# Half of a first MLP stage as seven half-size products instead of eight, with its x sums on VectorE

## Chip, cores and metric

One NeuronCore of a Trainium2 chip runs the whole program. The metric is the device time of one execution in microseconds; the time before is a median of 265.79 us over three runs (265.69 to 265.80). Views and rows call the engines PE (TensorE, matrix products), PEld (its weight loads), DVE (VectorE), ACT (ScalarE), POOL (GpSimd) and SP (SyncE, which here only issues DMAs).

## What is computed

```python
q_s = exp(q - max(q));  q_s /= sum(q_s, axis=-1)          # q, k, v: batch 8, heads 8, seq 576, head_dim 64
k_s = exp(k - max(k));  k_s /= sum(k_s, axis=seq)
kv  = einsum('bhsd,bhse->bhde', k_s, v)
x   = einsum('bhsd,bhde->bhse', q_s, kv)  ->  (8, 576, 512)
xn  = (x - mean(x)) / sqrt(var(x) + 1e-6) * g_ln
out = x + relu(xn @ w_ch1) @ w_ch2                        # w_ch1 (512, 2048), w_ch2 (2048, 512)
```

The output is float32 of shape (8, 576, 512).

## The kernel before

**Chunks.** The 8 x 576 rows of x are worked on in nine chunks of 512 rows: chunk c below 8 is the first 512 rows of batch c, chunk 8 (`C9`) the last 64 rows of all batches. A chunk has four column groups t of 128 rows. Attention gives x (`po_mm` on TensorE, then `x_fast` on VectorE, which scales x, sums it and calls `xn_out`), x is transposed to xnT (in chunk 1 by TensorE and a copy, `xn_pT`; from chunk 2 on by a DMA from SP's queue, `xn_T`), and the MLP follows in two stages. The first stage makes hT, 16 row tiles m of 128 rows, from w1g and xnT with four contraction steps ko; the second makes y from hT and w2.

**Order.** Everything is in a schedule written by hand: each engine executes its instructions in the order in which the program issues them. `run(main, side)` (L775) walks through a chunk's TensorE steps. Each has a weight, 1 for a matmul of 512 columns and 0.5 for one of 256, and before each step `run` issues all side work whose position is at most the weight so far. So "position 51" of chunk 1 means: behind 51 units of its main matmuls. `second_side` (L818) is the side work of chunk 1: the sums of the second weight for later products (`quarter_w2`), what is left of chunk 1 (`square_sum`, `rstd_op`), and the attention of chunk 2 and loads and exponentials of chunk 3. What a main step calls at its own end is issued within that step.

**Seven products.** From chunk 2 on, both stages replace eight products of half-size blocks by seven (a Strassen-Winograd form). `mm1_fast` (L691) does the first stage so: per g (four row tiles of hT, two block rows) seven products of four 256-column matmuls each, for pairs of g in the order 1, 5, 6, 2, 7, 3, 4, each product for both g of a pair before the next. It uses three PSUM banks per g, named x, b and c:

- after product 1, `seed` copies bank x to bank c (ScalarE); after 5, `copy_5` copies b to SBUF (ScalarE); after 6, `add_5` makes b = x + copy (VectorE, L719);
- after 2, a relu of c to hT (ScalarE); after 7, `out_22` writes x + copy to hT (VectorE, L722), for odd g with a maximum with 0 over two g (L727); after 3 and 4, relus of b and x (ScalarE).

Products 6, 7 and 4 add onto bank x, 2 onto c and 3 onto b, so 7 waits until `add_5` has read x, and 4 until `out_22` has. The products need sums of w1's blocks (`sum_w1`, in w1q, parts 0 and 1 for the lower and upper g) and of xnT's (`sum_x` into tq, four sums of two instructions each, L240: on GpSimd, or on VectorE from chunk 7 on).

The second stage `mm2_fast` (L622) does the same with 16 matmuls for each product in the order 1, 5, 6, 2, 7, 3, 4, and needs sums of hT (`sum_h(g, i)`, L528 on VectorE; g = 0 for hT's row tiles 0 to 7, g = 1 for 8 to 15). Product 5 reads sum 0, product 6 sum 1.

**Chunk 1 (`FAST`) before** uses seven products only in its second stage. Its first stage is `mm1_part` for row tiles 0 to 7 (64 matmuls of 256 columns, L451, with relus L462), columns t = 0 and 1 first since t = 3 is transposed at position 8, then `mm1` for row tiles 8 to 15 (32 matmuls of 512 columns, L436, relus L424): 64 units, and 56 for the second stage.

Six PSUM banks belong to the pool `mm_ps`, two to `att_ps` (kv and po).

Of the kernel before, what the change touches and what calls it, by code (L numbers as in the profile page):

```python
# [12 lines left out]
FP32 = mybir.dt.float32  # L13
# [7 lines left out]
def kernel(  # L21
# [16 lines left out]
    nc = tc.nc  # L38
# [5 lines left out]
    T = 4  # L44
# [183 lines left out]
    def sum_x(c, i):  # L228

        if i == 0:  # L230
            tqs[c] = mlp.tile([P, 4, 2, 2, P], BF16, tag="tq", name="tq", bufs=1)
        (b11, b12), (b21, b22) = [
            [xnTs[c][:, 2 * half : 2 * half + 2, 2 * kh : 2 * kh + 2, :] for half in range(2)]
            for kh in range(2)
        ]
        t1, t2, t3, t4 = [tqs[c][:, n] for n in range(4)]
        dst, x, y = ((t1, b12, b11), (t2, b22, t1), (t3, b22, b12), (t4, b21, t2))[i]
        eng = nc.vector if c >= C9 - 1 else nc.gpsimd
        for t in range(2):
            eng.tensor_tensor(out=dst[:, t], in0=x[:, t], in1=y[:, t], op=ALU.subtract)  # L240
# [178 lines left out]

    def relu(i, dst, src, fast):  # L420
        if i % 8 == 7 and not fast:
            nc.vector.tensor_scalar_max(dst, in0=src, scalar1=0.0)
        else:
            nc.scalar.activation(dst, src, AF.Relu)  # L424

    hbox = {}

    def new_h():
        hbox["h"] = mlp.tile([P, KO2, T, P], BF16, tag="hT", name="hT", bufs=1)

    def mm1(c, m, ko):
        if m == 0 and ko == 0:
            new_h()
        if ko == 0:
            hbox["ph"] = mm_ps.tile([P, T, P], FP32, tag="m", name="ph")
        nc.tensor.matmul(  # L436
            hbox["ph"], w1g[:, ko, m * P : (m + 1) * P], xnTs[c][:, :, ko, :],
            start=(ko == 0), stop=(ko == KO1 - 1),
        )
        if ko == KO1 - 1:  # L440
            relu(m, hbox["h"][:, m], hbox["ph"], c >= FAST)

    def mm1_part(c, m, t0, tn, ko):

        if (m, t0, ko) == (0, 0, 0):
            new_h()
        half, at = divmod(t0, 2)
        if m % 2 == 0 and at == 0 and ko == 0:
            hbox["ph", m // 2] = mm_ps.tile([P, 2, 2, P], FP32, tag="m", name="ph")
        ph = hbox["ph", m // 2]  # L450
        nc.tensor.matmul(  # L451
            ph[:, m % 2, at : at + tn], (w1g if c else w1_sb)[:, ko, m * P : (m + 1) * P],
            xnTs[c][:, t0 : t0 + tn, ko, :],
            start=(ko == 0 and m % 2 == 0 and at == 0), stop=(ko == KO1 - 1),
            skip_group_check=True,
        )
        if m % 2 == 1 and at + tn == 2 and ko == KO1 - 1:
            dst = hbox["h"][:, m - 1 : m + 1, 2 * half : 2 * half + 2]
            if c == 0 and half and (m // 2) % 2 == 1:
                nc.vector.tensor_scalar_max(dst, in0=ph, scalar1=0.0)  # L460
            else:
                nc.scalar.activation(dst, ph, AF.Relu)  # L462
# [19 lines left out]

    def mm2(c, t, ko):
        if ko == 0:
            hbox["pc"] = mm_ps.tile([P, DM], FP32, tag="m", name="pc")
        nc.tensor.matmul(
            hbox["pc"], hbox["h"][:, ko, t, :], w2_sb[:, ko, :],
            start=(ko == 0), stop=(ko == KO2 - 1),
        )
        if ko == KO2 - 1:  # L490
            y_out(c, t, hbox["pc"])

    def mm2_stream(c, t, ko):
# [23 lines left out]
    def sum_h(g, i):  # L517

        if g == 0 and i == 0:
            hbox["s"] = mlp.tile([P, 4, KH, 2 * P], BF16, tag="hs", name="hs", bufs=1)  # L520
        ks = slice(KH // 2 * g, KH // 2 * g + KH // 2)
        s1, s2, s3, s4 = [hbox["s"][:, n, ks] for n in range(4)]
        a11, a12, a21, a22 = [h_part(odd, half, ks) for half in range(2) for odd in range(2)]
        dst, x, y, op = (
            (s1, a21, a22, ALU.add), (s2, s1, a11, ALU.subtract),
            (s3, a11, a21, ALU.subtract), (s4, a12, s2, ALU.subtract),
        )[i]
        nc.vector.tensor_tensor(out=dst, in0=x, in1=y, op=op)  # L528

    def prod(n, bank, t, k, first=False, own=False):  # L530

# [10 lines left out]
        else:  # L542
            rhs = w2_q[:, {5: 0, 6: 1, 7: 2, 4: 3}[n], k]
        nc.tensor.matmul(hbox[bank][:, t], lhsT, rhs, start=first and (own or t == 0) and k == 0,  # L544
                         stop=k == KH - 1, skip_group_check=True)
# [76 lines left out]
    def mm2_fast(c):  # L622
# [3 lines left out]
        def product(n, name, first=False, at=None, ts=range(2), own=False, cut=None):  # L626
            at = at or {}
            order = [(t, k) for t in ts for k in range(KH)]
            if cut:
                order = [(t, k) for ks in (range(cut), range(cut, KH)) for t in ts for k in ks]  # L630
            for i, (t, k) in enumerate(order):

                def go(t=t, k=k, i=i):
                    if i == 0 and first:
                        bank(name)
                    prod(n, name, t, k, first or own, own)
                    for fn in at.get(i + KH * ts[0], []):
                        fn()

                steps.append((0.5, go))  # L640
# [16 lines left out]
        def sums(*which):  # L657
            return [lambda g=g, i=i: sum_h(g, i) for g, i in which if g or c == FAST or i > 1]

        product(1, "a", first=True, cut=6, at={  # L660
            0: sums((1, 0), (0, 1), (1, 1)),
            15: [seed_c]})
# [27 lines left out]

    def mm1_fast(c):  # L691

# [44 lines left out]
        )  # L737
        steps.append((0, new_h))
        for g0 in (0, 2):
            for n, name, first, after in plan:  # L740
# [4 lines left out]
    def mlp_steps(c):  # L745
        if c > FAST:
            return mm1_fast(c) + mm2_fast(c)
        full = range(KO2)
        first, parts = [], ()
        if c == 0:  # L750
            full = range(0)
            parts = ((0, 2, 0, 1), (0, 2, 1, 1), (2, 2, 0, 1), (2, 2, 1, 1), (4, 4, 0, 2), (0, 4, 2, 1),
                     (0, 4, 3, 1), (4, 4, 2, 2), (8, 4, 0, 2), (8, 4, 2, 2), (12, 4, 0, 2), (12, 4, 2, 2))
        else:
            full, parts = range(8, KO2), ((0, 8, 0, 2), (0, 8, 2, 2))
        for m0, mn, t0, tn in parts:
# [3 lines left out]
            ]  # L760
        first += [(1, lambda m=m, ko=ko: mm1(c, m, ko)) for m in full for ko in range(KO1)]
        if c == 0:
# [3 lines left out]
            ]  # L766
        if c >= FAST:
            return first + mm2_fast(c)
        return first + [(1, lambda t=t, ko=ko: mm2(c, t, ko)) for t in range(T) for ko in range(KO2)]

# [47 lines left out]
    def second_side():  # L818
# [3 lines left out]
        s += [(3, lambda: exp_q(2, 0, 4)), (7, lambda: exp_q(2, 2, 4)), (7.2, lambda: eq_T(2))]  # L822
        s += [(42, lambda: square_sum(1, 2)), (67, lambda: square_sum(1, 3)), (71, lambda: rstd_op(1))]
        s += [(7.3, lambda: load_batch(3, (2,), eqTs[2][0:1, T - 1, NP - 1, 0:4])), (31, lambda: load_batch(3, (0,)))]
        s += [(9 + 2 * j, lambda j=j: cast_v(2, j)) for j in range(2)]
        s += [(7.4, lambda: load_v(3))]
        s += [(93 + j, lambda j=j: cast_v(3, j)) for j in range(2)]
        s += [(15 + 3 * t, lambda t=t: reduce_q(2, t, 2)) for t in (0, 2)]
        s += [(36, lambda: recip_q(2))]
        s += [(18, lambda: exp_k(2, 0, 4)), (22, lambda: exp_k(2, 2, 4)), (26, lambda: prep_kvrem(2))]  # L830
        s += [(41, lambda: kv_all(2))]
        s += [(46, lambda: start_x(2))]
        for t, (p0, p1) in enumerate(((52, 54), (57, 59), (62, 65), (70, 74))):
            s += spread([lambda t=t, i=i: po_mm(2, t, i) for i in range(NP)], p0, p1)
            s += [(p1, lambda t=t: x_fast(2, t)), ((73, 82, 88, 94)[t], lambda t=t: square_sum(2, t))]
        s += [(60, lambda: xn_T(2, 0, 2)), (77, lambda: xn_T(2, 2, 2)), (100, lambda: rstd_op(2))]
        s += [(75, lambda: exp_q(3, 0, 4)), (79, lambda: exp_q(3, 2, 4)), (85, lambda: eq_T(3))]
        s += [(97, lambda: exp_k(3, 0, 4)), (108, lambda: exp_k(3, 2, 4)), (113, lambda: prep_kvrem(3))]
        s += [(p, lambda i=i: sum_w1(i, 1)) for i, p in ((3, 30),)]
        s += spread([lambda i=i: sum_x(2, i) for i in range(4)], 95, 108)  # L840
        return s
# [184 lines left out]
    with tc.manual_schedule(  # L1026
# [10 lines left out]
        def po_x(c, t):  # L1037
# [25 lines left out]
            + [(p, lambda i=i: sum_w1(i, 0)) for i, p in enumerate((80, 84, 88, 92))]  # L1063
            + [(p, lambda i=i: sum_w1(i, 1)) for i, p in enumerate((96, 98, 100))]
            + [(103 + 0.4 * j, lambda j=j: cast_v(1, j)) for j in range(2)]
# [8 lines left out]
        for c in range(1, B):  # L1074
# [12 lines left out]
            if c == B - 2:  # L1087
                side += [(1, load_qrem)]
                side += spread([lambda r=r: exp_qrem(r) for r in range(T)], 58, 80)
                side += [(84, lambda: eq_T(C9))]  # L1090
            sums = [(57, 0)] if c == FAST else [(p, i) for i, p in enumerate((30, 41))]
            run(mlp_steps(c), side + [(at, lambda i=i: sum_h(0, i)) for at, i in sums])
# [31 lines left out]
```

## Time and profile before

| what | value |
|---|---|
| median of three runs | 265.79 us |
| the profiled execution | 265.6 us |
| its span, first to last instruction | 263.6 us |
| granted TensorE clock, mean | 0.999 |
| chunk 1's matmuls, both stages | 49.37 to 77.47 us |
| first row of the page's slices, PE | 9 of 10 in nearly every slice |

The page's parts are busy times by engine, the span in 40 slices, DMA queues, the chain of work that ended last, the costliest groups of instructions and the DMA issues. A busy PE is not a PE at its peak, since matmuls overlap in the pipeline; what tells is the distance between starts. In the rows "L719" is line 719 of the kernel, "out<-in" gives the tiles by their names in the program, and the bracket at the end of a timeline row is the idle time of the engine ahead of it and what ended it.

### The profile page before, as it was taken

To read this page: it belongs to the slowest core of one execution; us is meant where nothing else is said; L and a number is where in the kernel's file an instruction comes from. 1 tells how busy PE (TensorE), PEld (TensorE's weight loads), DVE (VectorE), ACT (ScalarE), POOL (GpSimd) and SP (SyncE) were. 2 spreads that over 40 slices of the span, in tenths; PEclk is the share of its full clock that TensorE was granted. 3 is DMA by queue.
4 is the path that set the end of the run, shared out by engine and by line. 5 is a ranking of instruction groups with operands and counts; after the bars stand their busy time and mean duration, and the time that the engine had idled before them with its cause. 6 is when DMAs were issued, how large, how long until landed. Compare 5 with 4: busy or idle time off the path is not lost.

```text
span 263.6 us, 6818 instructions
## 1 busy us (share of the span) xinstructions
PE 257.4 (98%) x2708; PEld 218.1 (83%) x2711; DVE 217.4 (82%) x475; ACT 178.8 (68%) x350; POOL 76.0 (29%) x126
## 2 busy tenths in 40 slices
PE   8989999999999999999999999999999999999993
PEld 5778855775988998899889988998899888888882
DVE  4667797968989997989798979997999889877873
ACT  4467852896966888688868886788678377438400
POOL 8652316203049007600760076008200300030000
PEclk9999999999999999999999999999999999999999
DMA  6999999997986995799879957997804620521014
GB/s 219 256 204 208 338 208 315 271 155 233 207 151 197 325 136 97 197 308 155 93 215 298 139 99 237 297 135 146 256 6 79 161 82 12 71 90 72 0 42 119
DMA packets 69847, 45.00 MB, mean 171 GB/s; under 512 B 41460, under 2 KB 66040, under 8 KB 69816
## 3 DMA queue, kind: packets, MB, share of 16 engines
q1 hardware_dynamic: 48896, 21.76, 39.3%
q0 software_dynamic: 20320, 22.29, 38.9%
q10 hardware_dynamic: 600, 0.53, 0.6%
q8 instruction: 21, 0.34, 0.6%
q14 instruction: 10, 0.08, 0.1%
HBM read 36.70 MB, written 9.44 MB: 175 GB/s over the span
## 4 chain that ended last, share of the span: by engine, by line
PE 92%; DMA 4%; POOL 2%; issue 0%; ACT 0%; DVE 0%; POOLq 0%
PE ba L544 21%; PE bx L688 19%; PE bb L688 9%; PE ph L451 8%; PE bb L544 5%; PE be L544 5%; PE bc L544 5%; PE pc L497 5%; PE bc L688 5%; DMA w_raw<-in_moe_w_ch_dram 4%; PE ph L436 3%; PE po L353 3%; PE pkv L316 2%; PE ptr L860 1%; POOL v L931 1%; PE po L360 1%
## 5 line engine op out<-in xcount | busy, mean ns | idle before, releaser
L544 PEld LDWEIGHTS <-hs 128*128 128x128 bf16 x512 | 49.5, 98 | 5.7
L688 PEld LDWEIGHTS <-w_q 128*128 128x128 bf16 x448 | 43.1, 98 | 5.2 <-issue 0.2
L544 PEld LDWEIGHTS <-hT 128*128 128x128 bf16 x384 | 37.2, 98 | 4.4
L240 POOL TENSOR_TENSOR tq<-xnT 128x256 bf16<-128x256 bf16 x20 | 12.9, 661 | 78.6 <-DMA xnT<-xn 47.2
L688 PEld LDWEIGHTS <-w1g 128*128 128x128 bf16 x336 | 32.2, 98 | 3.9
L544 PE MATMUL ba<-w_q,hs 128*128 128x256 bf16 x256 | 31.7, 273 | 0.0
L688 PE MATMUL bx<-tq,w_q 128*128 128x256 bf16 x224 | 29.0, 273 | 0.0
L561 POOL DMA_DIRECT2D out_dram<-ot x28 | 15.3, 557 | 46.4 <-DVE ot L555 46.4
L367 ACT ACTIVATE scrap<-x,mv 128x512 bf16<-128x512 bf16 x36 | 25.9, 719 | 1.7 <-DVE x L383 1.3
L383 DVE SCALAR_TENSOR_TENSOR x<-po,rq 128x512 bf16<-128x512 f32 x34 | 23.3, 685 | 1.2 <-PE po L353 1.1
L712 ACT COPY bc<-bx 128x512 f32<-128x512 f32 x28 | 15.2, 594 | 13.0 <-PE bx L688 13.0
L719 DVE TENSOR_TENSOR bb<-bx,s 128x512 f32<-128x512 f32 x28 | 18.2, 694 | 6.3 <-ACT s L716 6.3
L730 ACT ACTIVATE hT<-bc 128x512 bf16<-128x512 f32 x28 | 15.3, 595 | 11.9 <-PE bc L688 11.9
L202 DVE TENSOR_REDUCE zq<-eq 128x16 f32<-128x1024 bf16 (+1 forms) x20 | 20.6, 1049 | 2.3 <-ACT eq L193 2.3
L528 DVE TENSOR_TENSOR hs<-hT 128x1024 bf16<-128x1024 bf16 x32 | 20.9, 674 | 0.9 <-ACT hT L730 0.5
L730 ACT ACTIVATE hT<-bb 128x512 bf16<-128x512 f32 x28 | 15.2, 595 | 8.8 <-PE bb L688 8.8
L353 PE MATMUL po<-kv_sb,eqT 128*128 128x128 bf16 x120 | 20.5, 219 | 0.0
L722 DVE TENSOR_TENSOR hT<-bx,s 128x512 bf16<-128x512 f32 x28 | 18.0, 684 | 3.0 <-PE bx L688 3.0
L569 ACT COPY s<-ba 128x512 f32<-128x512 f32 x15 | 8.7, 579 | 12.5 <-PE ba L544 7.8
L544 PE MATMUL ba<-w_sb,hT 128*128 128x256 bf16 x128 | 16.7, 273 | 0.0
L544 PE MATMUL bb<-w_q,hs 128*128 128x256 bf16 x128 | 16.6, 273 | 0.0
L497 PE MATMUL pc<-w_sb,hT 128*128 128x512 bf16 x61 | 15.6, 379 | 0.2
(135 smaller groups left out, 536.9 us busy)
## 6 DMA issues: line engine op xcount, KB each, us to landing
out_dram<-ot POOLq DMA_DIRECT2D x32, 256.0 KB, 5.9
qt<-in_q_dram SPq DMA_DIRECT2D x5, 1024.0 KB, 7.1
kt<-in_k_dram SPq DMA_DIRECT2D x5, 1024.0 KB, 15.0
vt<-in_v_dram POOLq DMA_DIRECT2D x7, 512.0 KB, 14.3
w_sb<-in_moe_w_ch_dram POOLq DMA_DIRECT2D x4, 512.0 KB, 16.1
qt<-in_q_dram POOLq DMA_DIRECT2D x2, 1024.0 KB, 14.8
kt<-in_k_dram POOLq DMA_DIRECT2D x2, 1024.0 KB, 14.3
w_raw<-in_moe_w_ch_dram POOLq DMA_DIRECT2D x3, 512.0 KB, 13.1
```

The lines of the kernel that those rows point to most:

```text
L202: nc.vector.reduce_sum(eqs[c][1][:, ts], eqs[c][0][:, ts], axis=AX.X)
L353: nc.tensor.matmul(pobox["p"][:, i * P : i * P + P], eqTs[c][:, t, i, :], kv_sb[:, c, i, :], start=True, stop=True,)
L367: nc.scalar.activation(scrap, x[:, t], AF.Square, bias=mv[:, t, 0:1], scale=-float(DM), accum_out=mv[:, t, 1:2],)
L383: nc.vector.scalar_tensor_tensor(x[:, t].rearrange("p (h d) -> p h d", h=H), in0=pobox[c, t].rearrange("p (h d) -> p h d", h=H), scalar=1. ...
L451: nc.tensor.matmul(ph[:, m % 2, at : at + tn], (w1g if c else w1_sb)[:, ko, m * P : (m + 1) * P], xnTs[c][:, t0 : t0 + tn, ko, :], start=( ...
L497: nc.tensor.matmul(hbox["pc", t], hbox["h"][:, ko, t, :], w2_sb[:, ko, :], start=(ko == 0), stop=(ko == KO2 - 1),)
L528: nc.vector.tensor_tensor(out=dst, in0=x, in1=y, op=op)
L544: nc.tensor.matmul(hbox[bank][:, t], lhsT, rhs, start=first and (own or t == 0) and k == 0, stop=k == KH - 1, skip_group_check=True)
L688: nc.tensor.matmul(dst[:, q], lhsT, rhs, start=first and q == 0 and ko == 0, stop=ko == 1, skip_group_check=True)
L719: nc.vector.tensor_tensor(out=at[g, "b"], in0=at[g, "x"], in1=at[g, "s"], op=ALU.add)
L722: nc.vector.tensor_tensor(out=h_out(g, 1, 1), in0=at[g, "x"], in1=at[g, "s"], op=ALU.add)
L730: nc.scalar.activation(h_out(g, odd, half), at[g, name], AF.Relu)
```

## The change

For chunk 1 alone:

- `mlp_steps`: the first stage computes row tiles 8 to 15 by `mm1_part` (64 matmuls of 256 columns as before, of other rows), and then row tiles 0 to 7 by `mm1_fast(c, (0,))`, one pair of g: 56 matmuls of 256 columns, 28 units. `mm1`, `relu` and `mm2` have no caller left and go.
- x's four sums are issued at position 8.2, on VectorE. tq's sums for chunk 2 stay on GpSimd.
- `sum_h` for g = 1 is issued at 36 and 38, as those row tiles are now ready first; the second stage takes their rows first (`rows`), and the sums for g = 0 follow at its first step.
- Of `second_side`, what lay at 41 or later mostly moves 3 to 4 units sooner, as the first stage is 4 units shorter: `kv_all(2)` 41 to 38.5, `po_mm` and `x_fast` of chunk 2, `xn_T`, `exp_q`, `exp_k`, `cast_v`, `sum_x(2)`, `square_sum(1, 3)`, `rstd_op`. `quarter_w2` at 44 and 46 and `square_sum(1, 2)` at 42 stay.
- The last `sum_w1` of part 1 moves from position 30 of chunk 1 to 105 of chunk 0.

A flag in `prod` (which matmul clears its bank) is passed in another way, with the same effect for the other chunks.

```diff
-        eng = nc.vector if c >= C9 - 1 else nc.gpsimd
+        eng = nc.vector if c >= C9 - 1 or c == FAST else nc.gpsimd
...
-            order = [(t, k) for t in ts for k in range(KH)]
+            rows = [(k + KH // 2) % KH for k in range(KH)] if c == FAST else list(range(KH))
+            order = [(t, k) for t in ts for k in rows]
...
         product(1, "a", first=True, cut=6, at={
-            0: sums((1, 0), (0, 1), (1, 1)),
+            0: sums((0, 0), (0, 1)) if c == FAST else sums((1, 0), (0, 1), (1, 1)),
...
-    def mm1_fast(c):
+    def mm1_fast(c, pairs=(0, 2)):
...
-        for g0 in (0, 2):
+        for g0 in pairs:
...
         else:
-            full, parts = range(8, KO2), ((0, 8, 0, 2), (0, 8, 2, 2))
+            parts = ((8, 8, 0, 2), (8, 8, 2, 2))
...
-        first += [(1, lambda m=m, ko=ko: mm1(c, m, ko)) for m in full for ko in range(KO1)]
...
-        if c >= FAST:
-            return first + mm2_fast(c)
-        return first + [(1, lambda t=t, ko=ko: mm2(c, t, ko)) for t in range(T) for ko in range(KO2)]
+        return first + mm1_fast(c, (0,)) + mm2_fast(c)
...
-        s += [(42, lambda: square_sum(1, 2)), (67, lambda: square_sum(1, 3)), (71, lambda: rstd_op(1))]
+        s += [(42, lambda: square_sum(1, 2)), (63, lambda: square_sum(1, 3)), (67, lambda: rstd_op(1))]
...
-        s += [(93 + j, lambda j=j: cast_v(3, j)) for j in range(2)]
+        s += [(89 + j, lambda j=j: cast_v(3, j)) for j in range(2)]
...
-        s += [(41, lambda: kv_all(2))]
+        s += [(38.5, lambda: kv_all(2))]
         s += [(46, lambda: start_x(2))]
-        for t, (p0, p1) in enumerate(((52, 54), (57, 59), (62, 65), (70, 74))):
+        for t, (p0, p1) in enumerate(((49, 51), (54, 56), (59, 62), (66, 70))):
             s += spread([lambda t=t, i=i: po_mm(2, t, i) for i in range(NP)], p0, p1)
-            s += [(p1, lambda t=t: x_fast(2, t)), ((73, 82, 88, 94)[t], lambda t=t: square_sum(2, t))]
-        s += [(60, lambda: xn_T(2, 0, 2)), (77, lambda: xn_T(2, 2, 2)), (100, lambda: rstd_op(2))]
-        s += [(75, lambda: exp_q(3, 0, 4)), (79, lambda: exp_q(3, 2, 4)), (85, lambda: eq_T(3))]
-        s += [(97, lambda: exp_k(3, 0, 4)), (108, lambda: exp_k(3, 2, 4)), (113, lambda: prep_kvrem(3))]
-        s += [(p, lambda i=i: sum_w1(i, 1)) for i, p in ((3, 30),)]
-        s += spread([lambda i=i: sum_x(2, i) for i in range(4)], 95, 108)
+            s += [(p1, lambda t=t: x_fast(2, t)), ((69, 78, 84, 90)[t], lambda t=t: square_sum(2, t))]
+        s += [(57, lambda: xn_T(2, 0, 2)), (73, lambda: xn_T(2, 2, 2)), (96, lambda: rstd_op(2))]
+        s += [(71, lambda: exp_q(3, 0, 4)), (75, lambda: exp_q(3, 2, 4)), (81, lambda: eq_T(3))]
+        s += [(93, lambda: exp_k(3, 0, 4)), (104, lambda: exp_k(3, 2, 4)), (109, lambda: prep_kvrem(3))]
+        s += spread([lambda i=i: sum_x(2, i) for i in range(4)], 91, 104)
...
-            + [(p, lambda i=i: sum_w1(i, 1)) for i, p in enumerate((96, 98, 100))]
+            + [(p, lambda i=i: sum_w1(i, 1)) for i, p in enumerate((96, 98, 100, 105))]
...
-            sums = [(57, 0)] if c == FAST else [(p, i) for i, p in enumerate((30, 41))]
+            if c == FAST:
+                side += [(8.2, lambda i=i: sum_x(c, i)) for i in range(4)]
+                side += [(p, lambda i=i: sum_h(1, i)) for i, p in enumerate((36, 38))]
+            sums = [] if c == FAST else [(p, i) for i, p in enumerate((30, 41))]
```

## Prediction

> **What bounds the kernel now.** First the page's first part, then the busy time by stage (columns: stretch and its length, then busy time and count of PE, PEld, DVE, ACT, POOL, the granted TensorE clock, DMA share, GB/s). Its first row is chunk 1, its second chunk 2.
>
> ```profile
> PE 257.4 (98%) x2708; PEld 218.1 (83%) x2711; DVE 217.4 (82%) x475; ACT 178.8 (68%) x350; POOL 76.0 (29%) x126
> ```
>
> ```profile
> 49.37:77.47 28.10, 28.10 (x271) 22.10 (x269) 22.97 (x51) 24.05 (x47) 5.25 (x10) 1.00 1.09 209
> 77.47:103.68 26.21, 26.21 (x283) 23.44 (x281) 23.41 (x49) 20.59 (x39) 11.19 (x19) 1.00 0.86 190
> ```
>
> TensorE is busy for the whole of chunk 1, so whether it works or stands is read from the chain of waits (start, length, what). There eight 256-column matmuls take 0.87 us and nine 512-column ones 1.94 us:
>
> ```profile
> 51.34 5.24 PE ph L451 x48
> 56.58 1.94 PE ph L436 x9
> ...
> 79.22 0.87 PE bx L688 x8
> ```
>
> That is 0.109 us for a 256-column matmul, 0.218 us for one unit of the list's weight. 120 units (26.21 us), the 40 small matmuls of kv (0.84), 16 of po (0.87) and four transposes (0.22) make 28.14 us, against 28.10 measured: chunk 1 has no TensorE stall, and the end of the kernel hangs on TensorE's work.
>
> Then VectorE's own timeline in chunk 1, because the change gives VectorE work there (start, length of the merged group, instruction, count, idle time before and its releaser). Groups overlap their neighbours: what an instruction costs its queue is the distance to the next start, which I call its pitch.
>
> ```profile
> 51.38 0.42 DVE L864 COPY xnT<-ptr 128x512 bf16<-128x512 bf16 x1 [0.27 <-PE ptr L860]
> 51.72 0.68 DVE L511 TENSOR_TENSOR w_q<-w_sb 128x1024 bf16<-128x1024 bf16 x1
> 52.32 0.77 DVE L134 COPY vm<-vt 128x1024 bf16<-128x1024 bf16 x2
> 52.99 0.69 DVE L511 TENSOR_TENSOR w_q<-w_sb 128x1024 bf16<-128x1024 bf16 x1
> 53.59 2.34 DVE L202 TENSOR_REDUCE zq<-eq 128x16 f32<-128x1024 bf16 x2
> 55.85 0.75 DVE L226 TENSOR_TENSOR w_q<-w1g 128x512 bf16<-128x512 bf16 x2
> 56.52 0.35 DVE L804 RECIPROCAL rq<-zq 128x32 f32<-128x32 f32 x1
> ...
> 59.32 0.18 DVE L325 RECIPROCAL rzk<-pkv 128x4 f32<-128x4 f32 x1 [2.45 <-PE pkv L316]
> 59.54 0.86 DVE L327 TENSOR_TENSOR kv_sb<-pkv,rzk 64x256 bf16<-64x256 f32 x2
> 60.43 1.42 DVE L511 TENSOR_TENSOR w_q<-w_sb,w_q 128x1024 bf16<-128x1024 bf16 x2
> 62.45 0.69 DVE L383 SCALAR_TENSOR_TENSOR x<-po,rq 128x512 bf16<-128x512 f32 x1 [0.61 <-PE po L353]
> ```
>
> The reader sees two holes, 2.45 and 0.61 us. The rows that the added work is priced by stand in later chunks, and one on ScalarE:
>
> ```profile
> 56.86 1.13 ACT L462 ACTIVATE hT<-ph 128x512 bf16<-128x512 f32 x2
> ...
> 79.75 1.30 DVE L719 TENSOR_TENSOR bb<-bx,s 128x512 f32<-128x512 f32 x2 [0.23 <-ACT s L716]
> ...
> 82.30 1.29 DVE L722 TENSOR_TENSOR hT<-bx,s 128x512 bf16<-128x512 f32 x2 [0.28 <-PE bx L688]
> 83.63 0.70 DVE L727 TENSOR_SCALAR hT<-hT 128x1024 bf16<-128x1024 bf16 x1
> ...
> 205.14 0.49 DVE L240 TENSOR_TENSOR tq<-xnT 128x256 bf16<-128x256 bf16 x2 [0.87 <-DMA xnT<-xn]
> ```
>
> **TensorE's part.** 32 matmuls of 512 columns (weight 32) go, 56 of 256 columns (weight 28) come: 4 units, 4 x 0.218 = 0.87 us less. Without a new wait the median would be 265.79 - 0.87 = 264.92.
>
> **Work that lies beside other work.** ScalarE loses eight L424 and gets ten copies and relus of the same size (0.59 us); walked on from 57.82 (the pitch after the L462 pair) the two seeds and two copies of product 5 end at 59.9, while VectorE first wants them at 60.3: hidden with 0.4 us to spare; without that cover a delay would pass one to one into `add_5` and on to TensorE. The last `sum_w1` (two instructions, 0.67) goes into VectorE's 0.85 us wait for pkv ahead of 42.85: nothing, and 0.67 late for `x_fast(1, 0)` without that wait. The y stores, loads and transposes keep their order on SP and POOL. POOL waits until 59.35 for the transposed eq before load 3, which nothing of this delays. `xn_T(2, 0, 2)` on SP waits for the second `x_fast`, about 1.5 us later than before by the walk below, the second transpose about 0.4; POOL's sums at 75.94 so start at most 1.5 late, their first is done by 78.8 and the shifted chunk 2 needs it at 79.1.
>
> **VectorE's part**, walked in program order. TensorE's due times come from 51.34 (position 8) + 0.218 per unit, + 0.84 for kv at 38.5, + 0.055 for each po matmul. Start of each piece, then pitch:
>
> - 51.38 copy 0.34; 51.72 x's sums, 8 instructions: the group that starts at 205.14 is followed by three like it, the last ends its pitch at 206.77, so 1.63; 53.35 two quarters, two casts 1.87; 55.22 two reduces 2.26; 57.48 reciprocal 0.27.
> - 57.75: `sum_h(1, 0)` needs the last relu of rows 8 to 15, which the L462 row ends at 57.99. So x's sums fit into the old 2.45 us hole; 0.28 us of it is left. Two sums of 0.605: 58.03 to 59.24.
> - 59.24: kv's reciprocal and products, 1.11 (59.32 to 60.43 above): to 60.35. So far VectorE is where it was before, but the hole is used up and four additions stand ahead of what used to follow.
> - `add_5` of g = 0 and 1: the L719 pair has pitch 0.605, result after 0.69. Results at 61.04 and 61.65. Product 7 of g = 0 is due at 60.92: **TensorE waits 0.12**, g = 1 another 0.03.
> - Two quarters (60.43 to 61.84 before, pitch 1.33): from 61.56 to 62.89. `out_22` of g = 0 result 63.58 (L722: pitch 0.605, result 0.68). TensorE, after products 7 and 3 and eight po, comes to product 4 of g = 0 at 63.28: **waits 0.30**. Product 4 adds onto bank x, which out_22 must have read.
> - `x_fast(2, 0)` at 51 is queued between the two out_22 (that of g = 0 comes in the step at 49.5, that of g = 1 in the one at 51.5): 1.01 (62.45 to 63.46), from 63.49 to 64.50. `out_22` of g = 1 result 65.18. TensorE wants product 4 of g = 1 at 64.01: **waits 1.17**.
>
> Queued behind it: the maximum (0.34 to 0.62 by the two cases in chunk 2), `x_fast(2, 1)` 1.01, `sum_h(0, 0)` 0.605, done at 67.3. TensorE starts product 4 of g = 1 at 65.2, then product 1 with five po, and reaches product 5, the sum's reader, at 67.72, so that holds. Before, product 5 began at 66.94 (its first matmul; VectorE's sums were ready at 66.3).
>
> **Sum.** Product 5 of the second stage 0.78 us later: waits of 0.12 + 0.03 + 0.30 + 1.17 = 1.62, plus 0.03 of latency at the last one, less 0.87. Afterwards VectorE is due later than it works: `add_u` to bank e can start at 72.2 and is read at 74.9; the v casts end a wait for DMA at about 73.1 as before. Nothing gives the 0.78 back, since TensorE then has no hole to fill. The profiled execution took 265.6, of which 263.6 is span and 2.0 lies around it; its sum is 266.4, and the median, 0.19 above that execution, **266.57**.
>
> Unknown: how soon TensorE goes on after VectorE's result in this stage, which never occurs before. From below, 0 (VectorE goes on at 82.30 after a product whose fourth matmul ends its pitch at 82.27); from above 0.2, the wait of a transpose for xn in the first stage. I take 0.03, nearest to the same pair of engines and banks. And whether pitch or length counts for a VectorE instruction behind another kind: length for four additions would be 0.36 more. The forecast's own range is 266.3 to 267.0.
>
> **Rivals.**
> - *VectorE keeps up (other side).* If out_22 of g = 1 lands by 63.54, product 4 never waits and the 0.87 is all gained: 264.92. For it: DVE is idle for 5.1 us of chunk 1, and the additions sum to 3.7 (1.63 + 4 x 0.605 + 0.34 - 0.67). Against it: the large hole lies before 59.3 and the sums of x and h take it; 13.5 us of pitches stand between 51.38 and that result, 64.9 even without any wait. It decides from 1.65 us less than I count; 0.78 us less gives no change.
> - *Half of it.* If quarters and `x_fast` overlap more, or waits are shorter, 0.8 us of stall balances the gain: 265.8, the band 265.3 to 266.3. For it: lengths, not due times, are measured; against: every duration has its row.
> - *Banks.* The stage wants six mm_ps banks at once, x, c, b of two g, while the last two ph are released at about 57.5 and 58.0; b of g = 0 is due at 57.45. If it gets the bank freed last, product 5 and kv behind it slip 0.55, VectorE's kv_out with them: 267.1. For it: all six banks are in use; against: the bank freed first is handed out first wherever chunks meet without a stall.
> - *Clock.* TensorE with four gaps within 4.3 us could be granted half its clock; the 2.4 us of matmuls from product 4 through product 1 would take twice as long: 269.0. Against: the granted clock is 1.00 in the first 16 us, with 1.54 us of gaps. The Trainium skill, "TensorE: Matmul & The Clock Gate" (HAM oscillation), puts the limit at gaps of more than about 3.4 us, longer than mine, and by it the clock holds; its next section reports drops from repeated micro-idles, which the trace before, at 1.00 throughout this stage, cannot show.
>
> **How the numbers follow.** Forecast 0.61, banks 0.13, half 0.12, VectorE keeps up 0.12, clock 0.02. About 0.2% (0.53 us) is what a measurement tells from no change. Slower by more, above 266.32: forecast 0.56 of its 0.61, banks, clock: 0.71. Within: the rest of the forecast and half: 0.17. Faster: 0.12. The range from 265.2 to 267.4 holds forecast, half and banks; it leaves out VectorE keeping up and the clock, 0.14. The likeliest one's own range is 266.3 to 267.0.
>
> **What would show it.** Right: PE's idle time before matmuls of bx names DVE for the first time, short at product 7, long (over 1 us) before the last bx group of chunk 1, with VectorE unbroken from 58.0 to that point, x_fast between the two L722; chunk 2 starts about 0.8 later than 77.47; chunks 2 to 9 keep 26.2. Wrong: no idle TensorE between 57 and 66 (VectorE kept up), or idle before bb of the first stage (banks), or a PEclk below 9 in that slice, or lost time in another chunk.

## The result, and the profile after

The changed kernel takes 266.75 us (median of 6 runs, 266.65 to 267.20) against 265.80 for the kernel before in the same comparison: ratio 1.0042, 95% interval 1.003 to 1.0055. Run a second time beside the experiments it gave 1.0055 (1.0043 to 1.0067). It is slower, by 0.95 and 1.45 us between the medians of the two comparisons. The profiled execution took 266.75 us, with a span of 264.7 (263.6 before).

The busy time by stage of the changed kernel (stretch, its length, then PE, PEld, DVE, ACT, POOL, clock, DMA share, GB/s): chunk 1, the two us before its last matmul group of bank x, and chunk 2.

```profile
49.22:78.57 29.35, 27.96 (x295) 24.41 (x293) 26.89 (x62) 25.03 (x49) 7.12 (x12) 1.00 1.02 201
...
63.10:65.30 2.20, 0.91 (x8) 0.52 (x6) 2.13 (x6) 1.48 (x3) 0.00 (x0) 1.00 0.98 324
...
78.57:104.78 26.21, 26.21 (x283) 23.44 (x281) 23.14 (x49) 20.58 (x39) 9.63 (x17) 1.00 0.94 189
```

Chunk 1 takes 29.35 us instead of 28.10, chunk 2 the same 26.21, and VectorE is busy for 3.9 us more in chunk 1. In 63.10 to 65.30 TensorE stands for more than half of the time while VectorE does not. TensorE's waits of the changed kernel name VectorE for bank x, which they never did before (us in total, times, longest):

```profile
PE bx L660 <- DVE hT L694: 1.3, 2, 1.0
```

TensorE's timeline of the changed kernel shows where (start, length, instruction; po rows left out; L660 is what was L688, L515 what was L544). Products of eight matmuls should start 0.87 us apart, and 0.055 later for each po between them.

```profile
56.27 1.04 PE L660 MATMUL bx<-xnT,w1g 128*128 128x256 bf16 x8
57.40 0.76 PE L660 MATMUL bb<-tq,w_q 128*128 128x256 bf16 x5
...
60.06 1.04 PE L660 MATMUL bc<-xnT,w1g 128*128 128x256 bf16 x8
61.06 0.38 PE L660 MATMUL bx<-tq,w_q 128*128 128x256 bf16 x2
...
62.15 0.60 PE L660 MATMUL bb<-xnT,w_q 128*128 128x256 bf16 x4
...
63.70 0.60 PE L660 MATMUL bx<-tq,w1g 128*128 128x256 bf16 x4 [0.29 <-DVE hT L694]
65.30 0.38 PE L660 MATMUL bx<-tq,w1g 128*128 128x256 bf16 x2 [1.00 <-DVE hT L694]
...
67.87 0.38 PE L515 MATMUL bb<-w_q,hs 128*128 128x256 bf16 x2
```

Distances, less the work between: product 1 to 5, 1.13 - 0.87 = 0.26 lost; 5 to 6 (rows not shown) 0.08; product 2 to 7, 1.00 - 0.87 = 0.13; product 3 to 4 of g = 0, 1.55 - 1.09 = 0.46; product 4 of g = 0 to g = 1, 1.60 - 0.44 = 1.16. Together 2.09 us lost against 0.87 saved: 1.22 of the 1.25 us by which chunk 1 is longer.

VectorE's timeline of the changed kernel in the same stretch, with no idle time in any row from 57.87 on (L499 the sums of h, L691 `add_5`, L482 the quarters, L694 `out_22`, L383 `x_fast`):

```profile
57.43 0.35 DVE L770 RECIPROCAL rq<-zq 128x32 f32<-128x32 f32 x1
57.87 0.69 DVE L499 TENSOR_TENSOR hs<-hT 128x1024 bf16<-128x1024 bf16 x1
58.60 0.69 DVE L499 TENSOR_TENSOR hs<-hs,hT 128x1024 bf16<-128x1024 bf16 x1
59.21 0.17 DVE L325 RECIPROCAL rzk<-pkv 128x4 f32<-128x4 f32 x1
59.41 0.86 DVE L327 TENSOR_TENSOR kv_sb<-pkv,rzk 64x256 bf16<-64x256 f32 x2
60.30 1.30 DVE L691 TENSOR_TENSOR bb<-bx,s 128x512 f32<-128x512 f32 x2
61.63 1.42 DVE L482 TENSOR_TENSOR w_q<-w_sb,w_q 128x1024 bf16<-128x1024 bf16 x2
62.97 0.68 DVE L694 TENSOR_TENSOR hT<-bx,s 128x512 bf16<-128x512 f32 x1
63.57 0.68 DVE L383 SCALAR_TENSOR_TENSOR x<-po,rq 128x512 bf16<-128x512 f32 x1
...
64.56 0.69 DVE L694 TENSOR_TENSOR hT<-bx,s 128x512 bf16<-128x512 f32 x1
```

The second out_22 ends at 65.25 (64.56 + 0.69), and product 4 of g = 1 starts at 65.30. Between the additions and the out_22 stand the two quarters, and between the two out_22 stands x_fast.

### The profile page after: what moved, and what is told of

Same layout as the page of the kernel before. It is cut to its first block, busy times and chain, and to the rows that moved or that the text cites. A ratio compares the mean times of both kernels' runs of the same rounds, so it can differ in the third digit from the quotient of the medians.

```text
span 264.7 us, 6888 instructions
## 1 busy us (share of the span) xinstructions
PE 255.8 (97%) x2732; PEld 219.6 (83%) x2735; DVE 221.6 (84%) x488; ACT 179.9 (68%) x352; POOL 76.3 (29%) x126
## 4 chain that ended last, share of the span: by engine, by line
PE 92%; DVE 4%; DMA 2%; ACT 1%; issue 0%; DVEq 0%; ACTq 0%
PE ba L515 21%; PE bx L660 19%; PE bb L660 9%; PE ph L432 8%; PE bb L515 5%; PE bc L515 5%; PE be L515 5%; PE pc L468 5%; PE bc L660 5%; PE po L353 2%; PE pkv L316 2%; DMA qt<-in_q_dram 2%; PE ptr L825 1%; PE warm L759 1%; PE z L274 1%; DVE hs L499 1%
## 5 line engine op out<-in xcount | busy, mean ns | idle before, releaser
L515 PEld LDWEIGHTS <-hs 128*128 128x128 bf16 x512 | 49.5, 98 | 5.7
L660 PEld LDWEIGHTS <-w_q 128*128 128x128 bf16 x480 | 46.1, 98 | 5.9 <-issue 0.5
L515 PEld LDWEIGHTS <-hT 128*128 128x128 bf16 x384 | 37.1, 98 | 4.3
L660 PEld LDWEIGHTS <-w1g 128*128 128x128 bf16 x360 | 34.5, 98 | 5.8 <-issue 1.6
L515 PE MATMUL ba<-w_q,hs 128*128 128x256 bf16 x256 | 31.7, 273 | 0.0
L660 PE MATMUL bx<-tq,w_q 128*128 128x256 bf16 x240 | 31.3, 273 | 0.0
L684 ACT COPY bc<-bx 128x512 f32<-128x512 f32 x30 | 16.4, 599 | 13.0 <-PE bx L660 13.0
L691 DVE TENSOR_TENSOR bb<-bx,s 128x512 f32<-128x512 f32 x30 | 19.5, 695 | 6.7 <-ACT s L688 6.6
L383 DVE SCALAR_TENSOR_TENSOR x<-po,rq 128x512 bf16<-128x512 f32 x34 | 23.3, 685 | 0.6 <-PE po L353 0.5
L702 ACT ACTIVATE hT<-bb 128x512 bf16<-128x512 f32 x30 | 16.4, 595 | 9.8 <-PE bb L660 9.7
L694 DVE TENSOR_TENSOR hT<-bx,s 128x512 bf16<-128x512 f32 x30 | 19.4, 685 | 3.0 <-PE bx L660 3.0
L499 DVE TENSOR_TENSOR hs<-hT 128x1024 bf16<-128x1024 bf16 x32 | 20.9, 675 | 0.6 <-ACT hT L702 0.5
L702 ACT ACTIVATE hT<-bx 128x512 bf16<-128x512 f32 x30 | 16.5, 605 | 1.3 <-PE bx L660 1.3
L660 PE MATMUL bx<-tq,w1g 128*128 128x256 bf16 x120 | 15.8, 272 | 1.3 <-DVE hT L694 1.3
L688 ACT COPY s<-bb 128x512 f32<-128x512 f32 x30 | 16.8, 626 | 0.1
```

The lines of the kernel that those rows point to most:

```text
L383: nc.vector.scalar_tensor_tensor(x[:, t].rearrange("p (h d) -> p h d", h=H), in0=pobox[c, t].rearrange("p (h d) -> p h d", h=H), scalar=1. ...
L515: nc.tensor.matmul(hbox[bank][:, t], lhsT, rhs, start=start, stop=k == KH - 1, skip_group_check=True)
L660: nc.tensor.matmul(dst[:, q], lhsT, rhs, start=first and q == 0 and ko == 0, stop=ko == 1, skip_group_check=True)
L688: nc.scalar.copy(at[g, "s"], at[g, "b"])
L691: nc.vector.tensor_tensor(out=at[g, "b"], in0=at[g, "x"], in1=at[g, "s"], op=ALU.add)
L694: nc.vector.tensor_tensor(out=h_out(g, 1, 1), in0=at[g, "x"], in1=at[g, "s"], op=ALU.add)
```

## The experiments

Each is the changed kernel with an edit. The expectations weigh three theories: A, TensorE waits because of the order in VectorE's queue; B, VectorE has too much work in this chunk, whatever its order; C, the PSUM banks of the first stage come free too late. "Chunk 1" is the time from its first matmul to chunk 2's first, read from TensorE's timeline of one profiled execution; ratios are to the kernel before on the same chip, and are not exactly the quotients of the medians (median there 265.34 beside x_fast behind out_22, two quarters later, both moves and x's sums on GpSimd; 265.47 beside the changed kernel again, the two with ekr and the loads behind; 265.59 beside the third quarter and x's sums twice).

| run | chunk 1, us | median, us | ratio (95% interval) |
|---|---|---|---|
| kernel before | 28.10 | | 1 |
| changed kernel | 29.35 | 266.75 | 1.0042 (1.0030 to 1.0055) |
| the same again | 29.34 | 266.92 | 1.0055 (1.0043 to 1.0067) |
| x_fast behind out_22 | 29.22 | 266.72 | 1.0047 (1.0035 to 1.0058) |
| two quarters later | 28.19 | 265.65 | 1.0015 (1.0003 to 1.0028) |
| both moves | 28.06 | 265.37 | 0.9996 (0.9987 to 1.0005) |
| both, ekr later | 27.83 | 265.46 | 0.9998 (0.9989 to 1.0006) |
| both, ekr and po(2, 2) later | 27.61 | 265.13 | 0.9986 (0.9977 to 0.9995) |
| and a third quarter | 27.99 | 265.35 | 0.9990 (0.9978 to 1.0002) |
| x's sums twice | 30.72 | 268.10 | 1.0092 (1.0070 to 1.0114) |
| x's sums on GpSimd | 38.96 | 274.42 | 1.0338 (1.0309 to 1.0368) |
| x's sums on GpSimd, loads behind | 32.89 | 270.48 | 1.0199 (1.0176 to 1.0221) |

**The changed kernel again**, unchanged.

> The changed kernel, unchanged, beside the others on the same chip: chunk 1 takes 29.3 to 29.4, ratio 1.003 to 1.0055.

As expected: 29.34 us and 1.0055. Two profiles of the kernel agree in chunk 1 to 0.01 us, so chunk 1's time tells edits apart more sharply than the medians do: between the profiles of these runs the start of chunk 1 alone differs by up to 0.65 us (48.92 to 49.57).

**x_fast behind out_22.**

```diff
-            s += [(p1, lambda t=t: x_fast(2, t)), ...
+            s += [(p1 + (t == 0), lambda t=t: x_fast(2, t)), ...
```

> The changed kernel with x_fast(2, 0) one unit later (position 52 for 51), so that it is queued behind out_22 of g = 1 and its maximum. Theory A (order in VectorE's queue: product 4 waits for an out_22 that stands behind two quarters and one x_fast): out_22 of g = 1 is done 1.0 us sooner, at 64.25, product 4 of g = 1 waits some 0.1 to 0.2 instead of 1.2, but the second stage's product 5, then due at 67.0, waits until about 67.3 for its sum, which has the same work ahead of it as in the changed kernel: 0.7 less than 266.75, about 266.05. Theory B (load: VectorE has 3.7 us too much work in chunk 1, whatever its order): 266.75, the wait only moves. Theory C (PSUM banks of the first stage are late): 266.75, with the wait before product 5 of the first stage left as it is.

The 0.7 us did not come: 29.22. Waits, and then the chain of waits, of this run:

```profile
PE po L353 <- DVE x L383: 0.7, 1, 0.7
...
PE bx L660 <- DVE hT L694: 0.3, 1, 0.3
```

```profile
64.72 0.62 DVE x L383 x2
65.34 0.05 issue
65.39 0.23 PE po L353
```

out_22 of g = 1 now came nearly in time, as theory A had it, but the same product 4 has the first po(2, 2) in its middle, and this waits for an `att_ps` bank that x_fast(2, 0) has to release. I had overlooked that a po waits behind x_fast as product 4 does behind out_22. VectorE had almost the same work ahead of either, so the wait only changed its name. That is what theory B said of this run.

**Two quarters later.**

```diff
-        s = [(p, lambda i=i: quarter_w2(i, 1)) for i, p in enumerate((8.5, 13, 44, 46))]
+        s = [(p, lambda i=i: quarter_w2(i, 1)) for i, p in enumerate((8.5, 13, 60.5, 63))]
```

> The changed kernel with the last two quarter_w2 at 60.5 and 63 instead of 44 and 46, behind both out_22 and the sums for the second stage's product 5. Theory A: both out_22 come 1.33 us sooner, product 4 of g = 0 does not wait (0.45 less), that of g = 1 waits 0.2 instead of 1.2, and the sum for product 5 is in time: 1.3 less, about 265.45. Theory B: 266.75, since no work is taken away, only moved within the chunk. Theory C: 266.75.

Chunk 1 is 1.16 us shorter, close to the 1.3 of theory A; theories B and C expected nothing. No work was taken from VectorE; it was put behind what TensorE waits for.

**Both moves.**

> Both moves: x_fast(2, 0) at 52 and the two quarters at 60.5 and 63. Theory A: product 4 waits for neither out_22; what is left are some 0.1 at product 7 and 0.3 at product 5 of the first stage: 1.6 less than 266.75, about 265.15, which is 0.65 below the kernel before. Theory B: 266.75. Theory C: 266.75.

28.06: product 4 waits for no out_22 any more. On top of the quarters' move, moving x_fast is worth 0.13 us. Of the expected 1.6 us 1.3 came, because the po bank takes part of it. TensorE's timeline of this run has one wait left that it names, 0.31 us of distance:

```profile
64.08 0.23 PE L353 MATMUL po<-kv_sb,eqT 128*128 128x128 bf16 x1 [0.15 <-DVE x L383]
```

**Both moves, and ekr later.**

```diff
-        s += [..., (26, lambda: prep_kvrem(2))]
+        s += [..., (32.2, lambda: prep_kvrem(2))]
```

> Both moves of before (x_fast(2, 0) at 52, quarters at 60.5 and 63), and prep_kvrem(2), a ScalarE exponential of 0.46 us, at 32.2 instead of 26, behind the last relu of rows 8 to 15. With both moves alone chunk 1 took 28.06 us from its first matmul to chunk 2's first (28.10 in the kernel before, 29.35 in the changed one), and TensorE still lost 0.26 before product 5 (bank b), 0.13 before product 7 and 0.31 before po(2, 2). Theory C' (bank b of the first stage waits for ScalarE to release a ph bank, which has that exponential in front): the relus come 0.3 sooner, the 0.26 and the 0.13 go, chunk 1 takes 27.7. Rival (the gap before product 5 is the wait for x's sums or a switch of weights): 28.06 stays.

27.83. (ekr is the tile that this exponential writes.) TensorE's timeline of this run, products 1 and 5:

```profile
56.13 1.04 PE L660 MATMUL bx<-xnT,w1g 128*128 128x256 bf16 x8
57.00 0.71 PE L660 MATMUL bb<-tq,w_q 128*128 128x256 bf16 x5
```

The first product 5 now follows product 1 after 0.87 us instead of 1.13, so the 0.26 was the bank; product 7 went on waiting, 0.2. The rival is out for the gap before product 5, since neither x's sums nor the weights were moved. The ratio does not resolve a step of this size.

**Both moves, ekr and po(2, 2) later.**

```diff
-        for t, (p0, p1) in enumerate(((49, 51), (54, 56), (59, 62), (66, 70))):
+        for t, (p0, p1) in enumerate(((49, 51), (54, 56), (60, 63), (66, 70))):
```

> As the run with prep_kvrem(2) at 32.2, and po(2, 2) at 60 to 63 instead of 59 to 62, so that it need not wait for x_fast(2, 0) to release its att_ps bank. If product 4's waits, the bank of product 5, product 7 and po are all that keeps the change from its 0.87 us: chunk 1 takes 27.2 to 27.3, the ratio to the kernel before is about 0.997 (0.8 us less). If VectorE's load limits, a new wait appears, most likely product 5 of the second stage for its sum, and the time stays at that of the kernel before.

27.61 against 28.10, and the one version that is faster than the kernel before beyond its interval, by 0.05 to 0.23%. In the trace 0.5 of the 0.87 us are gained, between the medians 0.34. VectorE's timeline of this run, and TensorE's, whose product 7 follows product 2 (60.26) by 1.08:

```profile
57.94 0.35 DVE L770 RECIPROCAL rq<-zq 128x32 f32<-128x32 f32 x1
58.21 0.63 DVE L499 TENSOR_TENSOR hs<-hT 128x1024 bf16<-128x1024 bf16 x1
...
60.59 1.30 DVE L691 TENSOR_TENSOR bb<-bx,s 128x512 f32<-128x512 f32 x2
```

```profile
61.34 0.38 PE L660 MATMUL bx<-tq,w_q 128*128 128x256 bf16 x2
```

The sums of h now follow the reciprocal at once (0.27 us, its pitch): VectorE's own queue, not the relus, sets add_5.

**And a third quarter.**

```diff
-        s = [(p, lambda i=i: quarter_w2(i, 1)) for i, p in enumerate((8.5, 13, 60.5, 63))]
+        s = [(p, lambda i=i: quarter_w2(i, 1)) for i, p in enumerate((8.5, 65, 60.5, 63))]
```

(and po(2, 2) at 61 to 64.)

> As the run with all four moves (chunk 1 took 27.61 us there, with 0.21 lost before product 7 and 0.1 at po(2, 2)), with a third quarter_w2 moved from 13 to 65 and po(2, 2) at 61 to 64. There VectorE was unbroken from 51.7 to add_5, so by theory A 0.6 us less ahead of it lets the sums of h start with the last relu again: product 7 waits at most 0.1, po(2, 2) not at all, chunk 1 takes 27.25 to 27.35, ratio about 0.997. If instead something other than VectorE's queue sets product 7's start (ScalarE's copy, the bank), 27.5 to 27.6 stays.

Product 7 lost 0.13 instead of 0.21, and the second stage's product 5 came 16.89 us after the chunk's start instead of 17.08. But chunk 1 took 27.99: the second stage's product 7 now waits. TensorE's and VectorE's timelines of this run:

```profile
72.08 1.92 PE L515 MATMUL ba<-w_q,hs 128*128 128x256 bf16 x16 [0.34 <-DVE hs L499]
```

```profile
69.13 0.68 DVE L482 TENSOR_TENSOR w_q<-w_sb 128x1024 bf16<-128x1024 bf16 x1
...
70.73 1.29 DVE L499 TENSOR_TENSOR hs<-hT 128x1024 bf16<-128x1024 bf16 x2
```

The moved quarter stands ahead of the sums that this product reads. From 57.88 to 76 VectorE's timeline names 0.2 us of idle time. This fits theory B: with the order mended, the load is the limit, and moved work turns up at the next due time. It is one order only; no run shows that every other one fails.

**x's sums twice.**

```diff
-                side += [(8.2, lambda i=i: sum_x(c, i)) for i in range(4)]
+                side += [(8.2, lambda i=i: sum_x(c, i)) for i in (0, 1, 2, 3, 1, 2, 3, 2)]
```

> The changed kernel with four of x's sums (numbers 1, 2, 3, 2) computed a second time on VectorE at 8.2: 8 more instructions, 1.63 us. Theory A: the hole behind the first sums was 0.17 us (VectorE free at 57.70, sums of h from 57.87), so the rest, 1.46 us, goes through to product 4 one to one: chunk 1 takes 30.8 us against 29.35, ratio about 1.0097. If VectorE's extra work early in the chunk is hidden elsewhere (a rival in which the wait before product 4 has another cause, such as the kv products or ScalarE), 29.4, ratio 1.0045.

30.72 against 30.8 expected. All but a quarter of a us of the added 1.63 reaches the end. TensorE's timeline of this run:

```profile
62.82 0.38 PE L660 MATMUL bx<-tq,w_q 128*128 128x256 bf16 x2 [1.34 <-DVE bb L691]
...
67.06 0.38 PE L660 MATMUL bx<-tq,w1g 128*128 128x256 bf16 x2 [0.99 <-DVE hT L694]
```

The added time is taken at product 7, which waits for add_5, and not at product 4, where it was expected; the waits at product 4 stay what they were (0.99 beside 1.00). Early work on VectorE was free only up to that quarter: the hole of 0.17 us that x's sums had left, and 0.07 between the two sums of h, which start 0.66 apart in this run instead of 0.73. Theory B gives a longer time for this run too, so it speaks only against the rival in which early work is hidden.

**x's sums on GpSimd.**

```diff
-        eng = nc.vector if c >= C9 - 1 or c == FAST else nc.gpsimd
+        eng = nc.vector if c >= C9 - 1 else nc.gpsimd
```

> The changed kernel with x's sums for chunk 1 on GpSimd at the same position 8.2 instead of VectorE: 1.63 us of VectorE's work gone, some 5.1 us of GpSimd's from 51.6 to 56.7 added. Theory A: these sums lay in the hole ahead of the sums of h, which wait for the last relu of rows 8 to 15 (57.84) anyway; nothing behind them moves by more than 0.1: 266.65 to 266.75. Theory B: VectorE is 1.63 us less loaded, so 1.3 to 1.6 less: about 265.2 to 265.4. Theory C: 266.75. A GpSimd that is late would show as a wait of product 5 or 6 of the first stage for tq and a longer time.

The times of all three theories missed: 38.96. Only the sign named for a late GpSimd came, product 5 waiting for tq. The profiled execution is the slowest of the six (276.42 us). GpSimd's timeline of this run, then TensorE's waits:

```profile
60.73 0.18 POOL L985 CAST qt<-eqT 1x4 f32<-1x4 bf16 x1 [7.46 <-DMA eqT<-eq]
...
64.09 1.34 POOL L240 TENSOR_TENSOR tq<-xnT 128x256 bf16<-128x256 bf16 x2
```

```profile
PE bb L660 <- POOL tq L240: 8.2, 1, 8.2
```

The sums, issued at 8.2, stood behind load 3, issued at 7.3, whose first step waits on GpSimd for the transposed eq. I had priced them from 51.6 on without that wait. The wait of 8.2 us also cost TensorE half its clock for a while (last section). This run says nothing of A against B.

**x's sums on GpSimd, loads behind.** (The edit above, and:)

```diff
-        s += [(7.3, lambda: load_batch(3, (2,), ...
+        s += [(8.3, lambda: load_batch(3, (2,), ...
-        s += [(7.4, lambda: load_v(3))]
+        s += [(8.4, lambda: load_v(3))]
```

> The changed kernel with x's sums for chunk 1 on GpSimd, and load 3 (q, and v) issued at 8.3 and 8.4, behind these sums instead of ahead of them, so that the sums do not stand behind GpSimd's wait for the transposed eq. They run from about 51.6 to 56.7, ahead of that wait's end at 59.2. Theory A (order in VectorE's queue): the sums of h still start with the last relu at 57.84, chunk 1 takes 29.3 as in the changed kernel, ratio 1.004. Theory B (VectorE's load): 1.63 us less load, chunk 1 takes 27.7 to 28.1, ratio 0.998 to 1.000.

Missed again, 32.89, in another way: GpSimd now ran the sums from 52.98 to 58.04, and VectorE stood through them. GpSimd's and VectorE's timelines of this run:

```profile
52.98 1.31 POOL L240 TENSOR_TENSOR tq<-xnT 128x256 bf16<-128x256 bf16 x2
...
56.75 1.29 POOL L240 TENSOR_TENSOR tq<-xnT,tq 128x256 bf16<-128x256 bf16 x2
```

```profile
52.31 6.03 DVE L134 COPY vm<-vt 128x1024 bf16<-128x1024 bf16 x2
58.25 0.68 DVE L482 TENSOR_TENSOR w_q<-w_sb 128x1024 bf16<-128x1024 bf16 x1
```

Two casts that take 0.76 us together in the changed kernel took 6.03, the second of them 5.69, ending at 58.34, 0.3 us behind the last of GpSimd's eight instructions; add_5 came 3.4 us later, counted from the chunk's start. So taking the sums off VectorE did not lighten it, and A against B is not decided by this run either; the moves decide it.

## Why the prediction was right, point by point

- **What bounds the kernel**: right. Chunks 2 and later keep 26.21 us, and TensorE's time in chunk 1 passes to the end one to one.
- **TensorE's saving of 0.87**: right in the account above, where 2.09 us lost less 0.87 leave 1.22 of the measured 1.25.
- **The place and cause of the new wait**: right. Product 4 waits for out_22, VectorE is unbroken from 57.87, x_fast stands between the two out_22. That this order is the cause is shown by the two moves: 29.35 to 28.19 and 28.06 with the same work. Of the two things that stand ahead, the quarters are what counts (1.16 us): x_fast moved alone gave 0.13, because a po then waits for it at nearly the same time. The prediction's walk has no due time for x_fast itself.
- **x's sums in the hole**: right, 0.17 us of it left instead of 0.28. The doubling shows that the hole is then used up.
- **The size**, the term that was mis-sized: waits of 2.09 instead of 1.65 us, a shift of 1.25 in the trace instead of 0.78 (0.95 between the medians of the first comparison). Three parts make up most of it. The due times were taken from the chain of waits, where a running matmul starts 0.16 us later than in TensorE's timeline (51.34 and 51.18 for the same group before), so that a standing TensorE had been due 0.16 sooner. VectorE was about 0.22 later than walked: the second sum of h reads the first, and that distance is 0.73 instead of 0.605; and the first quarter starts 0.03 behind the end of the second add_5 (60.30 + 1.30) and not at its pitch, another 0.12, of which the other pieces give back 0.02. And two po, not one, follow the start of product 4 of g = 1 ahead of the second stage, 0.05. Together they are 0.43 of the 0.47 between 0.78 and 1.25. That the forecast of 266.57 lies within 0.2 us of 266.75 is in part luck: the second comparison put the change at 1.45 us.
- **Banks**: the rival came true in part. Product 5 lost 0.26 us, for bank b, and the ekr move removed it. But it seems not to have been added to the rest, as I had it: VectorE's queue ran on meanwhile, and without the 0.26 product 4 would have waited by that much more. This is argued; no run moves ekr alone.
- **VectorE keeps up** and **half of it** did not come. How little was missing for the second shows in the move of the quarters, 28.19 against 28.10 in the kernel before.
- **Clock**: 1.00 over chunk 1 of the changed kernel, its waits included. In the two runs with a wait of 3.3 and of 8.2 us it did fall (below).
- **Later stages**: as predicted, nothing gave the time back. The later x_fast did not reach chunk 2: GpSimd's sums for it started at 75.47, sooner than the 75.94 before.

What stays open is the rest of the gain. With all four moves 0.5 of 0.87 us are there; the run with the third quarter suggests that VectorE's work in this chunk has to shrink for the rest, but that is not shown, since other orders were not tried. A version with less work on it was not found: both runs with x's sums on GpSimd failed for other reasons.

## What to carry to other kernels

Fewer matmuls shorten a TensorE-bound stage only if the engine that combines their parts can answer within their spacing, so count not the idle time of that engine but its queue, entry by entry, up to each due time. Work without a near due time belongs behind the entries that the critical engine waits for: moving two sums was worth 1.16 us in chunk 1's time, with the same work. And a wait that is removed may hide a second with the same cause, here a PSUM bank behind the same x_fast: list for each queued entry all that waits for it.

## What the runs showed of the hardware

- A GpSimd tensor_tensor and a VectorE copy of bf16 from SBUF to SBUF held each other up: in the run with the loads behind, the second cast took 5.69 us instead of 0.42 while GpSimd worked through eight instructions of 0.66 us; later in the same run, two of GpSimd's sums that began beside two such casts took 1.56 us instead of 1.30. Not all of VectorE's instructions are held: in the kernel before, VectorE's additions of y out of PSUM took 0.87 to 0.88 us for two while GpSimd made the eight sums for chunk 2 (from 75.94 on), as they did with GpSimd idle. The Trainium skill, "SBUF — State Buffer" (Who interferes with whom), tells of an exclusive lock of the port pair that both share, held for one instruction; the trace agrees with the exclusion, and here the loser waited through eight instructions in a row. Why the cast lost, although it starts at 52.65 (58.34 - 5.69) and the sums only at 52.98, the trace does not show.
- TensorE's granted clock fell to half behind a wait of 3.3 us, though not at once. The windows of the run with GpSimd's sums ahead of the loads: in the wait, behind it, and 1.4 us later.

```profile
61.20:64.60 3.40, 0.13 (x2) 0.00 (x0) 3.27 (x8) 0.88 (x2) 0.79 (x2) 1.00 1.04 289
64.60:66.00 1.40, 1.38 (x14) 1.23 (x15) 1.34 (x3) 0.00 (x0) 0.00 (x0) 0.91 1.30 187
66.00:67.80 1.80, 1.80 (x12) 1.40 (x11) 1.80 (x4) 0.60 (x1) 0.00 (x0) 0.50 1.12 208
```

In the run with x's sums on GpSimd, where TensorE stood from about 57.3 to 65.5, it fell during the wait: a mean of 0.77 over 8 us is about 4.3 us at 1.00 and the rest at 0.50. It came back at about 71.6, some 6 us after matmuls had resumed:

```profile
57.00:65.00 8.00, 0.29 (x3) 0.11 (x2) 1.38 (x2) 1.80 (x4) 3.25 (x6) 0.77 0.62 158
...
68.00:71.00 3.00, 3.00 (x15) 2.12 (x15) 2.20 (x5) 1.30 (x3) 1.14 (x2) 0.50 1.27 236
71.00:74.00 3.00, 3.00 (x31) 2.61 (x29) 2.90 (x7) 1.70 (x3) 0.00 (x0) 0.90 1.03 116
```

Waits of 1.0 to 1.34 us in the other runs left it at 1.00. This is in keeping with the limit of about 3.4 us in "TensorE: Matmul & The Clock Gate" of the Trainium skill (HAM oscillation). These runs have waits of up to 1.34 us that left the clock alone and one of 3.3 us that did not, and place the limit no more closely.
